# One half tile of a routed mixture of experts, run as a quarter tile in four groups of array columns

## The chip, the cores and the metric

The kernel runs on one core of a Trainium2 chip. The metric is the device time of one execution in microseconds; the time before is the median of three runs. Profiles show one execution each. The engines are named as in the profile: PE (matrix products) with PEld (its weight loads), DVE (vector), ACT (scalar), POOL (gather and scatter here) and SP (which sends the weight loads).

## The reference

A linear attention over 4 sequences of 768 tokens with 8 heads of 64 makes x, of 3,072 rows of 512. Each token then goes to one of 8 experts, and its row passes through that expert's two layers. What matters here, cut:

```python
logits = np.einsum('bsd,de->bse', x, w_gate)
local_gate = 1.0 / (1.0 + np.exp(-np.einsum('bsd,de->bse', x, w_local).squeeze(-1)))
for b in range(B):
    prev_e = -1
    for s in range(S):
        fresh_e = int(np.argmax(logits[b, s]))
        if s == 0 or local_gate[b, s] < 0.5:
            e = fresh_e
        else:
            e = prev_e if prev_e >= 0 else fresh_e
        prev_e = e
        ...
        h = np.maximum(x[b, s] @ w1[e], 0.0)
        out[b, s] = p[e] * (h @ w2[e])
```

w1[e] is 512 x 1024 and w2[e] is 1024 x 512, all in f32. p[e] is the token's softmax probability of its expert. The inputs come from a fixed seed, so the number of tokens of each expert is the same in every run. The kernel finds it on the chip all the same.

## The kernel before

**Attention and routing.** The first part goes through 24 steps, one for each block of 128 tokens (loop at L762). Each step computes scores (L181), the part from the running state (L216), the mix (L230), the update of the state (L242) and the rows of x (L258), which go to the DRAM tensor x_dram. Between the steps stand small pieces of other work, listed by step in the table extras (L732); constants_1 to constants_5 prepare constants there. A constant of this kind is dupb (L333): it copies rows 0 to 63 of a table to both halves of the 128 partitions when it is used as the stationary operand of a matmul.

**Tiles of tokens.** Tokens of one expert are collected in tiles of up to 128 rows. Five first tiles are taken while attention still runs. For the rest, other_tiles (L517) divides what each expert has left into pairs of tiles (256 rows, computed by a scheme of seven products in place of eight, L916), full tiles (128 rows) and half tiles (at most 64 rows). tokens_to_other_tiles (L544) gives each token its place and writes three numbers, arms[0] to arms[2]: how many later pairs, full tiles and half tiles there are. brought (L563) and by_slots (L580) turn places into row indices, gates and expert numbers for each tile. The numbers are read into registers (number, L727), and branches on them choose the code that runs (L1197 for the half tiles; the first arm, for three half tiles, falls through).

**A half tile.** Its rows come by a gather (ahead_half). turned_half (L1015) transposes them on PE. hidden_of_half (L1023) computes the first layer with the 64 tokens as the stationary operand, so that a matmul fills 64 of the 128 columns of the array; the outputs are cut in two, and the two cuts use columns 0 to 63 and 64 to 127. hidden_turned (L1033) transposes the result, and output_of_half (L1041) does the second layer in the same way, 8 steps of two matmuls. A row of 512 outputs so lies in two partitions, 256 values in each. both_halves (L612) prepares for this the scatter indices sidxh (two for each token) and the gates gateh. The scatter views out as rows of 256.

**Where half tiles run.** They have no stage of their own: hooks_of_halves (L1055) hangs their four steps into the first two pairs. With three half tiles, half 0 takes hooks 7 to 10 of pair 0, half 1 hooks 0 to 3 of pair 1, and half 2 hooks 7 to 10 of pair 1. Their weights have a set of buffers, w1t[2] and w2t[2]. The weights of the next half tile are sent by SP after the present one's last step, each layer once its reader on PE is done:

```python
            def end():
                output_of_half(h, now["ht"])
                if h + 1 < n:
                    weights_of(G2 + h + 1, 2)
```

**Order.** The orders of PE, DVE and SP are those of the program text (manual_schedule, L1105); each engine works through its own list and waits for what an instruction needs. Around the counts that order is: hiddens(2) and other_tiles, tokens_to_other_tiles, y of tile 2 (L724), brought (L568 and L577), then on PE by_slots (L587), which reads what L577 wrote. Constants written at steps 1 to 7 lie in ints, a region that the weights take later.

## Time and profile before

| measure | value |
|---|---|
| runs | 464.11, 515.61 and 462.61 us, median 464.11 |
| profiled execution | 462.59 us, of which the span from first to last instruction 460.4 |
| first half tile: L1018, L1027, L1036, L1046 | 195.66 to 209.6 us, with the pair's products between |
| second and third half tile, L1027 starts | 219.36 and 240.21 us |
| after the half tiles: third pair, full tiles, later pairs | from about 260 us to the end |
| last matmul of the span | starts 451.13, lasts 1.89 us |
| DMA moved | 124.30 MB, mean 270 GB/s |

Reading it: rows of the profile name a source line, an engine and the tile written and read. A piece of the chain of waits has its start and its length in microseconds. In an answer about a tile, three durations are the shortest, the median and the longest in nanoseconds.

### The profile page before, as it was taken

The numbers are of one execution on the slowest core, as the hardware profiler recorded it, in microseconds if no ns is written. First come the engines' busy times: TensorE is split into PE (matmuls) and PEld (weight loads), VectorE is DVE, ScalarE is ACT, GpSimd is POOL, SyncE is SP. The second block draws the span as 40 slices with busy tenths as digits, with TensorE's granted clock in tenths as the row PEclk, the third lists the DMA queues.
The fourth block names the chain that finished last, engine by engine and source line by source line (L and its number), as shares of the span: only waits on it lengthen the run. The fifth ranks groups of instructions, "written<-read, shape, count | busy, mean of one in ns | idle before, by whom it ended". The sixth has DMA issues, their size and how long they took to land.

```text
span 460.4 us, 10348 instructions
## 1 busy us (share of the span) xinstructions
PE 443.7 (96%) x4295; PEld 368.1 (80%) x4295; DVE 260.3 (57%) x514; ACT 111.4 (24%) x262; POOL 109.8 (24%) x121
## 2 busy tenths in 40 slices
PE   8898998989999999999999999999999999999993
PEld 7676886777766876968686999677799999898992
DVE  5465775762159743744373685100386877867661
ACT  3365665532011101121121031011031211213020
POOL 4475664421010120214021302010003012020101
PEclk9999999999999999999999999999999999999998
DMA  7999998996989999699993699997043828380101
GB/s 273 411 421 375 352 314 285 383 406 256 361 291 346 305 379 345 263 400 395 400 335 115 197 403 325 359 326 282 17 182 94 313 82 290 137 275 1 52 3 50
DMA packets 42236, 124.30 MB, mean 270 GB/s; under 512 B 3132, under 2 KB 3132, under 8 KB 40256
## 3 DMA queue, kind: packets, MB, share of 16 engines
q1 hardware_dynamic: 34544, 103.83, 61.5%
q0 software_dynamic: 4464, 14.16, 8.4%
q10 hardware_dynamic: 3168, 5.51, 3.2%
q8 instruction: 37, 0.61, 0.5%
q14 instruction: 23, 0.19, 0.1%
HBM read 123.49 MB, written 12.98 MB: 296 GB/s over the span
## 4 chain that ended last, share of the span: by engine, by line
PE 68%; DMA 15%; DVE 8%; issue 6%; POOL 1%; POOLq 0%; SPq 0%; ACT 0%; DVEq 0%
DMA xg<-x_dram,gidx 11%; PE pk L698 10%; PE ps L692 9%; PE ps L901 9%; PE pk L906 9%; DMA inp<-in_qkv_dram 4%; PE po L901 4%; PE pl L906 4%; PE po L237 4%; PE ps L197 3%; PE pr L1046 2%; PE pr L1027 2%; PE pk L261 2%; PE po L684 2%; PE po L224 2%
## 5 line engine op out<-in xcount | busy, mean ns | idle before, releaser
L692 PEld LDWEIGHTS ps<-xt,w 128*128 128x128 f32 x512 | 58.2, 192 | 3.4 <-issue 2.6
L692 PE MATMUL ps<-xt,w 128*128 128x128 f32 x512 | 59.1, 276 | 0.3 <-DVE xt L679 0.3
L698 PE MATMUL pk<-w,h 128*128 128x512 f32 x128 | 56.3, 592 | 0.0
L698 PEld LDWEIGHTS pk<-w,h 128*128 128x128 f32 x128 | 23.7, 190 | 26.8 <-issue 26.8
L669 POOL DMA_INDIRECT xg<-x_dram,gidx x23 | 25.5, 1110 | 78.4 <-PE po L684 57.9
L201 DVE TENSOR_TENSOR sm<-ps,mask 128x512 f32<-128x512 f32 x46 | 29.6, 685 | 16.9 <-PE ps L197 16.8
L707 POOL DMA_INDIRECT out_dram<-y,sidx x14 | 14.7, 1050 | 83.0 <-DVE y L724 46.5
L901 PE MATMUL ps<-xs,s 128*128 128x128 f32 x256 | 31.3, 275 | 0.1
L901 PEld LDWEIGHTS ps<-xp,w 128*128 128x128 f32 x256 | 30.4, 192 | 1.2 <-issue 0.9
L901 PE MATMUL ps<-xp,w 128*128 128x128 f32 x256 | 31.3, 275 | 0.0
L694 ACT ACTIVATE h<-ps 128x512 f32<-128x512 f32 x16 | 9.6, 597 | 88.0 <-PE ps L692 88.0
L906 PE MATMUL pk<-w,h 128*128 128x256 f32 x128 | 30.3, 379 | 0.0
L906 PE MATMUL pk<-s,hsum 128*128 128x256 f32 x128 | 30.2, 379 | 0.0
L901 PEld LDWEIGHTS ps<-xs,s 128*128 128x128 f32 x256 | 29.9, 192 | 0.3 <-DVE xs L882 0.3
L172 POOL TENSOR_TENSOR qd<-inp,lamq 128x512 f32<-128x512 f32 x20 | 25.6, 1280 | 16.4 <-DMA inp<-in_qkv_dram 4.4
L716 POOL DMA_INDIRECT out_dram<-y,sidxp x8 | 8.0, 1004 | 86.3 <-DVE y L997 80.4
L237 PE MATMUL po<-sm,inp 128*64 128x128 f32 x384 | 27.7, 280 | 0.8 <-issue 0.6
L724 DVE TENSOR_SCALAR y<-pk,gate 128x512 f32<-128x512 f32 x8 | 6.0, 746 | 39.7 <-PE pk L698 33.7
L237 PEld LDWEIGHTS po<-sm,inp 128*64 128x64 f32 x384 | 21.1, 136 | 8.3 <-issue 6.8
L175 POOL TENSOR_TENSOR kd<-inp,rev 128x512 f32<-128x512 f32 x20 | 21.7, 1084 | 20.6 <-PE pk L251 8.8
L906 PEld LDWEIGHTS pk<-s,hsum 128*128 128x128 f32 x128 | 24.0, 190 | 3.1
L906 PEld LDWEIGHTS pk<-w,h 128*128 128x128 f32 x128 | 23.2, 190 | 2.5
(258 smaller groups left out, 747.1 us busy)
## 6 DMA issues: line engine op xcount, KB each, us to landing
w<-in_w_dram SPq DMA_DIRECT2D x43, 2048.0 KB, 9.9
inp<-in_qkv_dram SPq DMA_DIRECT2D x15, 1024.0 KB, 9.0
x_dram<-xn ACTq DMA_DIRECT2D x21, 256.0 KB, 7.7
inp<-in_qkv_dram SPq DMA_DIRECT2D x10, 512.0 KB, 11.2
inp<-in_qkv_dram SPq DMA_DIRECT2D x4, 768.0 KB, 7.8
w<-in_w_dram SPq DMA_DIRECT2D x4, 512.0 KB, 8.0
x_dram<-xn POOLq DMA_DIRECT2D x2, 256.0 KB, 6.7
xg<-x_dram,gidx POOLq DMA_INDIRECT x23, 6.9
```

What stands on the lines that cost most here:

```text
L172: nc.gpsimd.tensor_tensor(qd, x[:, 0].rearrange("p (a i) -> p a i", i=P), lamq, ALU.mult)
L175: nc.gpsimd.tensor_tensor(kd.rearrange("p (h d) -> p h d", d=DH), x[:, 3].rearrange("p (h d) -> p h d", d=DH), rev.unsqueeze(2).broadcast_ ...
L197: nc.tensor.matmul(ps[u][half, a, first:], lhsT=kt[rows, a, js], rhs=qt[rows, a, first:], start=True, stop=True, skip_group_check=True)
L201: nc.vector.tensor_tensor(sm[:, u], ps[u], mask[:, u], ALU.mult)
L237: nc.tensor.matmul(head(a, u), lhsT=vn[:, a, u], rhs=sm[:, u, a], start=(not c and a < 2), stop=True, skip_group_check=True)
L669: nc.gpsimd.indirect_dma_start(out=xg, out_offset=None, in_=x_dram[:n, :], in_offset=bass.IndirectOffsetOnAxis(ap=gidx[i][:, j:j + 1], axi ...
L692: nc.tensor.matmul(ph[:, j], lhsT=w1t[w][:, d, P * f:P * f + P], rhs=xtt[i][:, d], start=(d == 0), stop=(d == DT - 1))
L694: nc.scalar.activation(hq[half, i], ph, ACT.Relu)
L698: nc.tensor.matmul(pys[i], lhsT=hq[f // 4, i][:, f % 4], rhs=w2t[w][:, f], start=(f == 0), stop=(f == FT - 1))
L707: apart(nc.gpsimd.indirect_dma_start(out=out, out_offset=bass.IndirectOffsetOnAxis(ap=sidx[i][:, j:j + 1], axis=0), in_=y, in_offset=None, ...
L901: nc.tensor.matmul(to[:, m], lhsT=a[:, k, P * m:P * m + P], rhs=b[:, k], start=(new and not m and not k), stop=(k == 1), skip_group_check= ...
L906: nc.tensor.matmul(to, lhsT=a[:, f], rhs=b[:, f], start=(new and not f), stop=(f == FT // 2 - 1), skip_group_check=True)
```

## The change

When there are three half tiles and the first of them has at most 32 tokens, that first one runs as a quarter tile: the 32 tokens are the stationary operand of four groups of 32 array columns, and each group computes a quarter of the outputs. A row of outputs then lies in four partitions, 128 values in each. For this there are a constant dupq (rows 0 to 31 copied four times) and fourth (the number of the quarter), a ninth column of sidxh and gateh, and a number FIRST_SMALL = 9 in arms[2] that the branch tests first. The case of three half tiles with a larger first one moves to the list of the other arms. The functions of a half tile take a number n of column groups, 2 or 4.

```diff
+QP = P // 4
+FIRST_SMALL = E + 1
...
+    def constants_6():
+        for k in range(4):
+            nc.vector.tensor_copy(dupq[:, QP * k:QP * k + QP], ident[:, :QP])
+        row = ints[0][:, 2 * P:2 * P + 1]
+        nc.vector.tensor_scalar(row, row, P - QP, None, ALU.bitwise_and)
+        nc.vector.tensor_scalar(fourth, row, 1.0 / QP, None, ALU.mult)
...
-    sidxh = route.tile([P, E], U32, name="sidxh")
-    gateh = route.tile([P, E], F32, name="gateh")
+    sidxh = route.tile([P, E + 1], U32, name="sidxh")
+    gateh = route.tile([P, E + 1], F32, name="gateh")
...
             nc.vector.tensor_tensor_scan(ends[:, k], ones8, tiles[:, k], float(g), ALU.mult, ALU.add)
-
+        small = nows["small"] = act.tile([1, E], F32, name="small", bufs=1)
+        nc.vector.scalar_tensor_tensor(small, rest[0:1], float(QP), tiles[0:1, 2], ALU.is_le, ALU.mult)
+        nc.vector.scalar_tensor_tensor(small, ends[0:1, 2], float(G2 + 1), small, ALU.is_equal, ALU.mult)
...
-        for k, g in ((1, G1), (2, G2)):
-            nc.vector.tensor_scalar(arms[k], ends[0:1, k, E - 1:], -float(g), None, ALU.add)
+        nc.vector.tensor_scalar(arms[1], ends[0:1, 1, E - 1:], -float(G1), None, ALU.add)
+
+        kind = act.tile([1, 3], F32, name="kind", bufs=1)
+        nc.vector.tensor_reduce(kind[:, 0:1], nows["small"], axis=AX.X, op=ALU.add)
+        nc.vector.tensor_scalar(kind[:, 1:2], ends[0:1, 2, E - 1:], -float(G2), None, ALU.add)
+        nc.vector.tensor_scalar(kind[:, 2:3], kind[:, 1:2], 3.0, float(FIRST_SMALL - 3), ALU.is_equal, ALU.mult)
+        nc.vector.scalar_tensor_tensor(arms[2], kind[:, 2:3], kind[:, 0:1], kind[:, 1:2], ALU.mult, ALU.add)
...
-        nc.tensor.matmul(twin, lhsT=dupb, rhs=nows["few"].rearrange("p k g -> p (k g)"), start=True, stop=True,
-                         skip_group_check=True)
+        nc.tensor.matmul(twin[:, :, :E], lhsT=dupb, rhs=few, start=True, stop=True, skip_group_check=True)
+        nc.tensor.matmul(twin[:, :, E:], lhsT=dupq, rhs=few[:, :, 0:1], start=True, stop=True, skip_group_check=True)
...
-        nc.vector.scalar_tensor_tensor(sidxh, src[:, 0], 2.0, upper.broadcast_to([P, E]), ALU.mult, ALU.add)
+        nc.vector.scalar_tensor_tensor(sidxh[:, :E], src[:, 0, :E], 2.0, upper.broadcast_to([P, E]), ALU.mult, ALU.add)
+        nc.vector.scalar_tensor_tensor(sidxh[:, E:], src[:, 0, E:], 4.0, fourth, ALU.mult, ALU.add)
...
-        (1, 0): constants_1, (4, 1): constants_2, (5, 1): constants_3, (6, 1): constants_4, (7, 1): constants_5,
+        (1, 0): constants_1, (4, 1): constants_2, (5, 1): constants_3, (6, 1): constants_4, (7, 1): constants_5, (8, 1): constants_6,
...
+        w = F // n
         for d in range(DT):
-            for c in range(2):
-                nc.tensor.matmul(pr[HP * c:HP * c + HP], lhsT=xt[:, d], rhs=w1t[2][:, d, F // 2 * c:F // 2 * c + F // 2],
+            for c in range(n):
+                nc.tensor.matmul(pr[P // n * c:P // n * c + P // n, :w], lhsT=xt[:, d], rhs=w1t[2][:, d, w * c:w * c + w],
                                  start=(d == 0), stop=(d == DT - 1), skip_group_check=True)
...
+        k = FT // n
         pt = pg.tile([P, DT, P], F32, name="po1")
-        for j in range(DT):
+        for j in range(k):
             nc.tensor.transpose(pt[:, j], hs[:, P * j:P * j + P], ident)
...
         for f in range(FT):
-            for c in range(2):
-                nc.tensor.matmul(py[HP * c:HP * c + HP], lhsT=ht[:, f % DT, f // DT],
-                                 rhs=w2t[2][:, f, DM // 2 * c:DM // 2 * c + DM // 2],
+            for c in range(n):
+                nc.tensor.matmul(py[P // n * c:P // n * c + P // n], lhsT=ht[:, f % k, f // k],
+                                 rhs=w2t[2][:, f, w * c:w * c + w],
                                  start=(f == 0), stop=(f == FT - 1), skip_group_check=True)
...
-        with tc.If(halves == 3, preferred_fallthrough_block=True, label="halves") as cmp:
-            first_pairs(3)
+        with tc.If(halves == FIRST_SMALL, preferred_fallthrough_block=True, label="halves") as cmp:
+            first_pairs(3, 4)
             others()
         with cmp.Else():
-            one_of(halves, [4, 2, 5, 1, 6, 0, 7, 8], None, first_pairs)
+            one_of(halves, [3, 4, 2, 5, 1, 6, 0, 7, 8], None, first_pairs)
             others()
```

More of the change, by code (lines that the diff above doesn't have):

```diff
@@ L299 @@
     upper = const.tile([P, 1], F32, name="upper")
+    dupq = const.tile([P, P], BF16, name="dupq")
+    fourth = const.tile([P, 1], F32, name="fourth")
     ones8 = const.tile([P, E], F32, name="ones8")
@@ L612, in both_halves @@
     def both_halves():
-        twin = pl[:, :5 * E]
-        nc.tensor.matmul(twin, lhsT=dupb, rhs=nows["few"].rearrange("p k g -> p (k g)"), start=True, stop=True,
-                         skip_group_check=True)
-        got = act.tile([P, 5, E], F32, name="twin", bufs=1)
-        nc.vector.tensor_copy(got, twin.rearrange("p (k g) -> p k g", k=5))
-        src = act.tile([P, 2, E], F32, name="srch", bufs=1)
+        twin = pl[:, :5 * (E + 1)].rearrange("p (k g) -> p k g", k=5)
+        few = nows["few"]
+        nc.tensor.matmul(twin[:, :, :E], lhsT=dupb, rhs=few, start=True, stop=True, skip_group_check=True)
+        nc.tensor.matmul(twin[:, :, E:], lhsT=dupq, rhs=few[:, :, 0:1], start=True, stop=True, skip_group_check=True)
+        got = act.tile([P, 5, E + 1], F32, name="twin", bufs=1)
+        nc.vector.tensor_copy(got, twin)
+        src = act.tile([P, 2, E + 1], F32, name="srch", bufs=1)
         nc.vector.tensor_scalar(src[:, 0], got[:, 0], -float(P), 0.0, ALU.add, ALU.max)
@@ L1013, in ahead_half, with turned_part @@
         collect(xgh, 1, G2 - KA + h)
-    def turned_half():
+    def turned_part(n):
         pt = pg.tile([P, DT, P], F32, name="po1")
@@ L1018, in turned_half, with hidden_of_part @@
             nc.tensor.transpose(pt[:, d], xgh[:, P * d:P * d + P], ident)
-        xt = act.tile([P, DT, HP], F32, name="xth", bufs=1)
-        nc.vector.tensor_copy(xt, pt[:, :, :HP])
-        return xt
-    def hidden_of_half(xt):
+        xt = act.tile([P, DT, HP], F32, name="xth", bufs=1)[:, :, :P // n]
+        nc.vector.tensor_copy(xt, pt[:, :, :P // n])
+        return xt
+    def hidden_of_part(xt, n):
+        w = F // n
         for d in range(DT):
-            for c in range(2):
-                nc.tensor.matmul(pr[HP * c:HP * c + HP], lhsT=xt[:, d], rhs=w1t[2][:, d, F // 2 * c:F // 2 * c + F // 2],
+            for c in range(n):
+                nc.tensor.matmul(pr[P // n * c:P // n * c + P // n, :w], lhsT=xt[:, d], rhs=w1t[2][:, d, w * c:w * c + w],
@@ L1028, in hidden_of_half, with hidden_turned @@
                                  start=(d == 0), stop=(d == DT - 1), skip_group_check=True)
-        hs = act.tile([P, F // 2], F32, name="hs", bufs=1)
-        nc.scalar.activation(hs, pr, ACT.Relu)
-        return hs
-    def hidden_turned(hs):
+        hs = act.tile([P, F // 2], F32, name="hs", bufs=1)[:, :w]
+        nc.scalar.activation(hs, pr[:, :w], ACT.Relu)
+        return hs
+    def hidden_turned(hs, n):
+        k = FT // n
         pt = pg.tile([P, DT, P], F32, name="po1")
-        for j in range(DT):
+        for j in range(k):
@@ L1036, in hidden_turned, with output_of_part @@
             nc.tensor.transpose(pt[:, j], hs[:, P * j:P * j + P], ident)
-        ht = act.tile([P, DT, 2, HP], F32, name="hth", bufs=1)
-        nc.scalar.copy(ht.rearrange("p j c i -> p j (c i)"), pt)
-        return ht
-    def output_of_half(h, ht):
-        py = pr[:, :DM // 2]
+        ht = act.tile([P, DT, P], F32, name="hth", bufs=1)[:, :k]
+        nc.scalar.copy(ht, pt[:, :k])
+        return ht.rearrange("p j (c i) -> p j c i", c=n)
+    def output_of_part(h, ht, n):
+        w = DM // n
+        k = FT // n
+        py = pr[:, :w]
@@ L1044, in output_of_half @@
         for f in range(FT):
-            for c in range(2):
-                nc.tensor.matmul(py[HP * c:HP * c + HP], lhsT=ht[:, f % DT, f // DT],
-                                 rhs=w2t[2][:, f, DM // 2 * c:DM // 2 * c + DM // 2],
+            for c in range(n):
+                nc.tensor.matmul(py[P // n * c:P // n * c + P // n], lhsT=ht[:, f % k, f // k],
+                                 rhs=w2t[2][:, f, w * c:w * c + w],
                                  start=(f == 0), stop=(f == FT - 1), skip_group_check=True)
-        y = act.tile([P, DM // 2], F32, name="yh", bufs=1)
@@ L1050, in output_of_half @@
-        nc.vector.tensor_scalar(y, py, gateh[:, h:h + 1], None, ALU.mult)
-        apart(nc.gpsimd.indirect_dma_start(out=out.rearrange("n (c d) -> (n c) d", c=2),
-                                           out_offset=bass.IndirectOffsetOnAxis(ap=sidxh[:, h:h + 1], axis=0),
-                                           in_=y, in_offset=None, bounds_check=2 * N - 1, oob_is_err=False))
-    def hooks_of_halves(n):
+        y = act.tile([P, DM // 2], F32, name="yh", bufs=1)[:, :w]
+        j = h if n == 2 else E
@@ L1057, in hooks_of_halves @@
+        nc.vector.tensor_scalar(y, py, gateh[:, j:j + 1], None, ALU.mult)
+        apart(nc.gpsimd.indirect_dma_start(out=out.rearrange("n (c d) -> (n c) d", c=n),
+                                           out_offset=bass.IndirectOffsetOnAxis(ap=sidxh[:, j:j + 1], axis=0),
+                                           in_=y, in_offset=None, bounds_check=n * N - 1, oob_is_err=False))
+    def hooks_of_halves(n, first):
         now = {}
@@ L1063, in steps @@
         def steps(h):
+            cols = 2 if h else first
             def start():
-                now["xt"] = turned_half()
+                now["xt"] = turned_part(cols)
                 if h + 1 < n:
@@ L1069, in middle @@
             def middle():
-                now["hs"] = hidden_of_half(now["xt"])
+                now["hs"] = hidden_of_part(now["xt"], cols)
             def turn():
-                now["ht"] = hidden_turned(now["hs"])
+                now["ht"] = hidden_turned(now["hs"], cols)
             def end():
-                output_of_half(h, now["ht"])
+                output_of_part(h, now["ht"], cols)
                 if h + 1 < n:
@@ L1105 @@
     with tc.manual_schedule(engines={PE, DVE, SP}):
-        more, fulls, halves = (number(k, n) for k, n in enumerate((PMAX - PMIN + 1, E + 1, E + 1)))
+        more, fulls, halves = (number(k, n) for k, n in enumerate((PMAX - PMIN + 1, E + 1, FIRST_SMALL + 1)))
         weights_of(KA, w_of(0), (2,))
@@ L1119, with first_pairs @@
         written(4, 0)
-        def first_pairs(n):
-            hooks = hooks_of_halves(n)
+        def first_pairs(n, first=2):
+            hooks = hooks_of_halves(n, first)
             def loads():
```

## The prediction

> **What bounds the kernel now.** I read the page first: busy shares, then slices.

> ```profile
> PE 443.7 (96%) x4295; PEld 368.1 (80%) x4295; DVE 260.3 (57%) x514; ACT 111.4 (24%) x262; POOL 109.8 (24%) x121
> ...
> PE   8898998989999999999999999999999999999993
> ...
> PEclk9999999999999999999999999999999999999998
> DMA  7999998996989999699993699997043828380101
> ```

> TensorE is busy in almost every slice at full clock, so a microsecond less of matmul is a microsecond less of span, unless something else is late in its place. DMA is the candidate: slices 15 to 20 (about 173 to 242 us), where the half tiles run, are nearly full. Next, the chain of waits from 195 to 211 us, which is the first half tile inside the first pair.

> ```profile
> 195.82 0.44 PE po L1018 x4
> 196.26 1.73 PE pk L906 x8
> 197.99 3.58 PE pr L1027 x16
> 201.57 0.59 PE po L684 x4
> 202.16 1.73 PE pl L906 x8
> 203.89 0.44 PE po L1036 x4
> 204.32 1.73 PE pk L906 x8
> 206.05 3.60 PE pr L1046 x32
> ```

> Every piece is TensorE, without a gap: transposes of the rows (L1018), first product (L1027), transposes of the hidden values (L1036), second product (L1046), with work of the pair between. An f32 matmul leaves two records, so x16 is 8 matmuls. No vector or scalar piece stands here, so what this tile saves on PE is saved. Then I read the chain and timeline around 140 to 157 us, where the tile counts are made:

> ```profile
> 149.51 0.13 DVE arm L559
> 149.64 0.12 DVE arm L561 x2
> 149.76 0.66 DVE y L724
> 150.42 1.03 DVE hit L568
> 151.45 0.02 issue
> 151.47 5.20 DVE w L577 x5
> 156.66 0.04 issue
> 156.71 2.17 PE pr L587 x24
> ```

> ```profile
> 156.71 2.17 PE L587 MATMUL pr<-w,lane 128*128 128x190 bf16 x24 [0.28 <-DVE w L577]
> ```

> Here VectorE is the chain, and PE already waits 0.28 us for it. Anything added to VectorE ahead of L577 is paid by PE at once.

> **Does the quarter run?** The reference's routing on its seeded inputs gives 410, 373, 371, 423, 434, 362, 354, 345 tokens for the experts. With 128 of each of experts 0 to 4 in the first five tiles and 256 of each in pairs, experts 0, 3 and 4 keep 26, 39 and 50; experts 5 to 7 take the full tiles. So three half tiles (the trace has three of each half group), and the first has 26 tokens, at most 32: arms[2] becomes 9 and the quarter arm runs.

> **First product.** Now 8 matmuls of 512 columns in two groups of 64 array columns. A full-width f32 matmul of 512 columns takes 0.86 us (L698, 16 records in 6.87 us), so 8 would need 6.87; two side by side took 3.58. After: 16 matmuls of 256 columns, each 0.43 us alone (L906, 8 records in 1.73), in four groups: 16 x 0.43 / 4 = 1.72, plus the fill that the half shows (3.58 - 3.44 = 0.14 to 0.18): 1.88. Gain 1.70. That four groups run side by side is seen in the gates, one matmul of 512 columns for each 32-column group:

> ```profile
> L275 PEld LDWEIGHTS pl<-xc,wgt x48: 106/108/109, 23.5 to 106.6; 128*32 128x32 f32 x48
> L275 PE MATMUL pl<-xc,wgt x48: 592/605/617, 23.5 to 107.0; 128*32 128x512 f32 x48
> ```

> On the chain one set (8 records) is 0.99 us at 39.82; four alone would be 3.44. That row never reloads a group's weights while its neighbours run; the quarter does, eight times in its second product. The half does it with two groups and loses nothing.

> **Second product.** Now 16 matmuls of 256 columns, 3.60 us; after, 32 of 128 columns in four groups. Alone each is 0.22 us (L692, 64 records in 7.14), 7.1 in all, / 4 = 1.79, plus fill: 1.90. Gain 1.70. The doubt is how fast instructions go in: 64 matmul records in 1.8 us is 28 ns each, each with a weight load. The nearest row is from_state:

> ```profile
> 48.51 0.45 PE po L224 x16
> ```

> 16 records in 0.45 us, 28 ns each. [...] L275 shows 3.44 / 0.99 = 3.5 including its fill, so mine (6.9 / 1.88 = 3.7, fill spread over more steps) leans on the row[...].

> **Transposes.** L1036: 4 become 2, each 0.147 (L684, four in 0.59): 0.29 gained. L1018 stays. Copies and gating off the path (relu 0.60, hth 0.59, yh 0.48, all on smaller tiles) get shorter; PE has a product of 1.73 us between each and its reader, so they bring nothing. The scatter (POOL, 1.02 us issue) stays one instruction with half the bytes.

> **Added on VectorE ahead of L577.** In the timeline independent small operations start about 0.08 apart, dependent ones 0.20:

> ```profile
> 140.14 0.17 DVE L530 SCALAR_TENSOR_TENSOR other<-other 128x8 f32<-128x8 f32 x1
> 140.34 0.17 DVE L531 TENSOR_SCALAR other<-other 128x8 f32<-128x8 f32 x1
> 140.42 0.32 DVE L533 TENSOR_TENSOR_SCAN ends<-ones,other 128x8 f32<-128x8 f32 x3
> ```

> small: one independent, one dependent, 0.28. kind: a reduction (0.08 to 0.15), an independent step, then two dependent ones, in place of one arm: net 0.5. Together 0.8 us, no cover, since PE already waits there. Behind it on VectorE stand y (L724), hit, w; POOL's gathers (160.5, 161.8) and SP's weight loads of 159.4 and 159.7 move with it, as do their users. Bounds: 0.5 (all pipelined at 0.08) to 1.3 (all at 0.2).

> **both_halves.** One more bf16 matmul with its load: L413 and L414 start 0.04 apart; 0.05 on PE. VectorE's extra operation (0.2) is covered: it sits idle 7.3 us before L881 at 181.8. Without that cover: 0.2.

> **constants_6.** Four casts of 128x32 and two single-column steps follow L254 at 44.1:

> ```profile
> 43.72 0.42 DVE L254 TENSOR_TENSOR kv<-pk,kv 128x256 f32<-128x256 f32 x1 [2.98 <-PE pk L251]
> 44.66 1.29 DVE L201 TENSOR_TENSOR sm<-ps,mask 128x512 f32<-128x512 f32 x2 [0.52 <-PE ps L197]
> ```

> Nearest is L335 (0.79 and 0.18, the long one beside a POOL operation) and L336 (0.21). About 1.0 us, of which 0.5 is the idle before L201. Behind it are the scores, then fresh_experts; the first reader on PE is L386 at 48.89, whose input L378 ends at 48.33. So 0.5 late costs 0 to 0.1; I take 0.1, bounds 0 and 0.6. The halves branch still falls through in its first arm, and no queue is passed by a moved step: counted from the tile's start, w1t[2] comes free 1.7 us earlier and w2t[2] 3.7.

> **Sum.** -1.70 - 1.70 - 0.29 + 0.80 + 0.05 + 0.10 = -2.75 us. The profiled execution took 462.59 (span 460.4 and 2.2 around it): 459.8. The runs were 462.61, 464.11 and 515.61; the median lies 1.5 above the profiled one, which would make 461.4. Two executions agree at 462.6, so I say 460.3.

> **Rivals.**
> Weights late: half 1's w1 is sent at 201.61, when L1027 frees the buffer, and read at 219.4; the interval shrinks from 17.8 to 15.8 us. Loads of 2048 KB land 9.9 us after issue in the median, so DMA can even stay as late as now (211.5) and miss nothing (needed at 215.7 at the earliest). Against: two loads around 160 us took 19.5 and 18.2, queued behind others. At 18.2 PE would wait 2.4 and leave 0.35: 462.2.
> [...]
> VectorE stretch worse than summed, 1.3 and 0.6 for the constants: gain 1.75, 460.8.
> Covers better than summed (0.5 and 0): 459.5.
> The other side: the four groups don't run side by side once each reloads its weights. In series the products take 6.9 and 7.1 us in place of 3.58 and 3.60; +6.8 - 0.29 + 0.95 = +7.5: 470.1, slower than before. It decides from an overlap of 2.1 of four downward (each product above 3.26 us). For: L275 does no reload. Against: the half's pair overlaps 1.92 of two with reloads.

> **Numbers.** Main case 0.60, weights 0.08, issue 0.13, VectorE 0.10, covers 0.05, series 0.04. The range 458.5 to 463.8 takes in all but the series case, with 1.5 us for where the median of a few runs falls. About 2% (9.3 us) is what a measurement of this kernel can tell from no change; no case reaches it on either side, and what I leave is for effects the profile doesn't show: faster 0.03, same 0.95, slower 0.02.

> **What would show it.** First product: 32 records in about 1.9 us at 195 to 200. Second: 64 in about 1.9; [...]near 7 series. L1036 x2. PE's idle before L587 from 0.28 to about 1.1, with L577 starting 0.8 later. L386 at most 0.1 later. No PE wait before half 1's L1027. The pairs and full tiles after 260 us keep their lengths and start about 2.7 earlier. I am wrong if the products take over 2.6 us each, or if a wait of over 1 us stands where the chain had none.

## The result, and the profile after

The changed kernel takes 460.65 us in the median of 13 runs (458.73 to 463.36) against 463.52 us before: a ratio of 0.9929, 95% interval 0.9904 to 0.9955. By the ratio that is 3.3 us less, between 2.1 and 4.4; the two medians differ by 2.87. It is under one percent, but clear of noise. One run of before, 515.61 us, was in a slow state and does not enter the ratio. The forecast was 460.3, by a sum of 2.75 us less.

The profiled execution took 462.44 us with a span of 460.7, and so hardly differs from the profiled one of before (462.59 and 460.4). The profiles show how both can be true. First the page of the changed kernel, its header and busy shares:

```profile
span 460.7 us, 10452 instructions
...
PE 442.0 (96%) x4342; PEld 368.2 (80%) x4342; DVE 261.8 (57%) x526; ACT 110.7 (24%) x262; POOL 110.0 (24%) x121
```

TensorE has 47 more records and 1.7 us less of busy time. The busy time alone decides little: second profiles of both kernels have 445.1 us before and 440.1 after. Next the chain of waits through the first half tile, which is now the quarter tile (start, length, what). L1048 is the first product, L1058 the transposes of the hidden values, L1070 the second product.

```profile
199.82 0.44 PE po L1038 x4
200.26 1.73 PE pk L926 x8
201.99 1.86 PE pr L1048 x32
203.85 0.59 PE po L704 x4
204.44 1.73 PE pl L926 x8
206.17 0.22 PE po L1058 x2
206.38 1.73 PE pk L926 x8
208.11 1.89 PE pr L1070 x64
210.00 0.59 PE po L704 x4
```

Read it against the chain shown in the prediction: 3.58 became 1.86, 0.44 became 0.22, 3.60 became 1.89, and the pair's own pieces between them kept their lengths. From the start of the first product to the end of the second it was 11.67 us and is 8.01: 3.66 less, all on the chain.

Then the price. The chain ahead of by_slots, and by_slots' line of the timeline with TensorE's wait in brackets:

```profile
153.07 0.05 DVE arm L572
153.13 0.06 DVE arm L573
153.19 0.07 DVE kind L576
153.25 0.07 DVE kind L577
153.33 0.02 issue
153.35 0.15 DVE kind L578
153.50 0.02 issue
153.53 0.04 DVE arm L579
153.56 0.10 issue
153.66 0.73 DVE y L744
```

```profile
160.68 2.17 PE L605 MATMUL pr<-w,lane 128*128 128x190 bf16 x24 [1.02 <-DVE w L595]
```

The wait of 0.28 us has become one of 1.02. The two rows of small stand earlier, at 143.88 and 144.05.

What hides all this in the profiled pair stands ahead of it. The transposes of the first expert tile (its turn, in the table), the first work behind attention that every version has, start at 104.20 in the changed kernel and at 100.97 before, in the chain 3.23 us later:

```profile
104.20 0.60 PE pr L698 x4
```

From there to the end of the span the changed kernel takes 356.50 us and the one before 359.43: 2.93 less. So the comparison needs two numbers for each profile, where this piece starts and how long the rest takes (the span less that start). All profiles of this study:

| kernel | turn of the first expert tile starts | from there to the end |
|---|---|---|
| before, two profiles | 100.97, 101.67 | 359.43, 359.43 |
| after, two profiles | 104.20, 98.95 | 356.50, 356.55 |
| additions only, two profiles | 101.69, 101.01 | 360.21, 360.19 |
| small and kind late | 102.15 | 355.75 |
| all counts and y late, two profiles | 101.80, 102.63 | 355.30, 355.47 |
| groups in turn | 103.33 | 363.17 |
| columns split | 102.43 | 356.57 |
| runs of two | 102.56 | 356.64 |
| before with constants_6 | 103.33 | 359.57 |

The second column scatters over 5 us, for one and the same kernel too; the third repeats within 0.2 us. What the change does inside the span is read from the third.

There is also a piece outside the span, the time of a run less its span. In every run of the kernel before with a span on record it is 2.06 to 2.24 us (median 2.12), and the same with constants_6 added. In every run of the versions with the whole change or all its additions it is 1.68 to 1.86 (median 1.75). So 2.9 us inside and 0.37 outside make the 3.3 of the ratio. The 0.37 comes with the additions other than constants_6, since the version without the quarter has it too; the cause was not looked for.

Inside and outside together give each version a ratio to compare with its runs, if the attention stage takes the same in the mean. The measured ratio agrees within its interval for the changed kernel, all counts late, groups in turn, constants_6 and the second run of the additions. It does not for the first run of the additions (1.0042, where 1.0009 is expected) and for small and kind late (0.9939, where 0.9913 is). Both come from the same series of runs, and so does groups in turn, which agrees.

### The profile page after: what moved, and what is told of

Read it like the earlier page. It is cut to its first block, busy times and chain, and to the rows that moved or that the text cites. A ratio compares the mean times of both kernels' runs of the same rounds, so it can differ in the third digit from the quotient of the medians.

```text
span 460.7 us, 10452 instructions
## 1 busy us (share of the span) xinstructions
PE 442.0 (96%) x4342; PEld 368.2 (80%) x4342; DVE 261.8 (57%) x526; ACT 110.7 (24%) x262; POOL 110.0 (24%) x121
## 4 chain that ended last, share of the span: by engine, by line
PE 70%; DMA 12%; DVE 9%; issue 7%; POOL 1%; POOLq 0%; ACT 0%; DVEq 0%
DMA xg<-x_dram,gidx 11%; PE pk L718 10%; PE ps L712 9%; PE ps L921 9%; PE pk L926 9%; PE po L239 5%; PE po L921 4%; PE ps L199 4%; PE pl L926 4%; PE pk L263 2%; PE pk L253 2%; PE pr L1070 2%; PE pr L1048 2%; PE po L704 2%; PE po L226 2%
```

## Experiments

**Before, a second profile.** No edit.

> The kernel before, profiled a second time. In the first pair of profiles everything up to the first matmul of the expert stage stood 3.2 us later after the change (pr L678 at 100.97 before, L698 at 104.20 after), though only constants_6 was added there. Theory A (the attention stage differs from execution to execution[...]): this piece starts anywhere from 100 to 105 us here too, at least 0.5 us away from 100.97. Theory B (constants_6 shifts that stage): it starts within 0.5 us of 100.97.

The turn starts at 101.67, 0.7 us from the first profile, which favours A, weakly. The rest of the table says more: one kernel, the changed one, started its turn at 104.20 and at 98.95. The last lies outside the 100 to 105 that I had allowed; the scatter is wider than stated. Whether constants_6 adds a small shift of its own can't be seen in such a scatter; the run with constants_6 alone, below, answers that.

**The additions without the quarter** (two runs).

```diff
-            first_pairs(3, 4)
+            first_pairs(3, 2)
```

> All additions of the change are kept and the branch of the ninth kind is taken, but its first half tile runs in two column groups as before. Theory A (the gain is the two products and two transposes of the quarter, 3.7 us, and the additions cost 0.8 to 0.95): slower than the kernel before by 0.8 to 0.95 us (ratio 1.002), 3.7 us slower than the changed kernel; products 3.58 and 3.60 us, TensorE waits about 1.0 us ahead of by_slots. Rival (the gain comes from what the branch or the layout of the code does, not from the quarter): as fast as the changed kernel, ratio 0.993.

Measured: ratio 1.0042 (1.0021 to 1.0063). The chain of this run has the products of a half tile back:

```profile
199.49 3.58 PE pr L1048 x16
203.07 0.59 PE po L704 x4
203.66 1.73 PE pl L926 x8
205.38 0.44 PE po L1058 x4
205.82 1.73 PE pk L926 x8
207.55 3.60 PE pr L1070 x32
```

and the wait ahead of by_slots stays:

```profile
158.18 2.16 PE L605 MATMUL pr<-w,lane 128*128 128x190 bf16 x24 [1.03 <-DVE w L595]
```

The rival is out: without the quarter nothing is gained. The table gives the additions 0.78 us and the quarter 3.71 (360.21 - 356.50). The runs, however, gave 1.9 us for the additions, with even the lower end of the interval, 1.0 us, above what the profile shows. So I repeated it.

> The additions without the quarter, once more, beside the changed kernel and the version with all counts late on one chip. By the profiles the stage behind attention is 0.8 us longer than before, but its runs were 1.9 us slower (1.0 to 2.9). Theory A (the attention stage varies by up to 3 us from execution to execution, and the runs of one call don't average that out): ratio nearer to 1.002 this time, interval with 1.0018 in it. Rival (the additions cost a further 1 us that the profiles don't show): ratio 1.004 again.

Measured: ratio 1.0008 (0.9988 to 1.0027), with 1.0018 in it, and 360.19 us from the turn to the end. The stage behind attention repeats to 0.02 us, while the ratio moved by 0.0034 between the two series of runs. Rival and first ratio are not confirmed. With the 0.37 us that the additions save outside the span they should cost 0.4 us in all, a ratio of 1.0009, and that is what the second series has. What the first series had more of isn't known.

**Constants_6 alone.** The kernel before, with

```diff
+        (8, 1): constants_6,
```

and its function, but no reader.

> The kernel before with nothing added but constants_6, whose results nobody reads. Theory A (covered: VectorE has 0.5 us free there and the next reader on TensorE has slack): four steps of the attention from the first L197 group after it keep their 10.95 us, ratio 1.000. Rival (the additions cost more in time, 1.9 us in the run with additions only, than the 0.8 that the stage behind attention shows, because of constants_6): the four steps take 0.5 us or more longer, ratio 1.002.

Measured: ratio 0.9993 (0.9971 to 1.0016). The chain's score pieces after it, and those of before, start and length:

```profile
45.07 0.81 PE ps L198 x24
49.00 0.81 PE ps L198 x24
52.55 0.81 PE ps L198 x24
56.02 0.81 PE ps L198 x24
```

```profile
43.77 0.81 PE ps L197 x24
47.70 0.81 PE ps L197 x24
51.24 0.81 PE ps L197 x24
54.72 0.81 PE ps L197 x24
```

10.95 us from the first to the fourth in both (three steps lie between them, where the expectation says four). On this stretch the constants cost nothing; the ratio alone would leave room for a loss of up to 0.7 us. Their cover is visible on VectorE, in the timeline of the changed kernel:

```profile
45.57 0.61 DVE L344 CAST dupq<-ident 128x32 bf16<-128x32 f32 x4
46.10 0.14 DVE L346 TENSOR_SCALAR w<-w 128x1 int32<-128x1 int32 x1
46.27 0.15 DVE L347 TENSOR_SCALAR fourth<-w 128x1 f32<-128x1 int32 x1
46.34 1.28 DVE L203 TENSOR_TENSOR sm<-ps,mask 128x512 f32<-128x512 f32 x2
```

0.8 us of work in the place of 0.5 us of idle time; sm starts 0.16 us later against its scores, and its reader on TensorE comes a step later.

**The counts late.** small and kind move behind brought, where VectorE waited for by_slots anyway (2.26 us ahead of its copy of the result, L609, in the changed kernel).

```diff
         brought(1, (0, 1, 2, 3, 4))
+        kind_of_first()
```

kind_of_first holds the six operations taken out of other_tiles and tokens_to_other_tiles.

> The changed kernel, with the four operations of kind and the two of small moved behind brought, where VectorE waits 2.26 us for by_slots. Theory A (the additions cost because VectorE is the chain ahead of by_slots): TensorE's wait ahead of by_slots falls from 1.02 to 0.25 to 0.35 us, the piece between the lane of the last tokens (VectorE) and by_slots is 0.7 to 0.8 us shorter than in the changed kernel, and the time is about 0.75 us below it (ratio to before 0.9915). Rival (the wait is set by something else, a load or the hidden product): the wait stays at 1.0 us.

```profile
157.72 0.15 DVE L576 SCALAR_TENSOR_TENSOR small<-other 1x8 f32<-1x8 f32 x1
157.85 2.17 PE L608 MATMUL pr<-w,lane 128*128 128x190 bf16 x24 [0.25 <-DVE w L598]
```

The wait is 0.25 us, and the rest takes 355.75 us, 0.75 less than in the changed kernel. The ratio, 0.9939 (0.9916 to 0.9963), does not show it: it is no lower than that of the changed kernel, and the 0.9915 that A had lies just outside its interval. By the profile A holds; by the runs it is not confirmed.

**All counts and y late** (two runs). In addition arms[0], arms[1] and the gating of the third tile go behind brought.

```diff
-        finished(2)
+        output(0, 0)
         weights(4)
         brought(1, (0, 1, 2, 3, 4))
         kind_of_first()
+        written(2, 0)
```

> The version with the late counts, with all three arms and the gating of the third tile (y, 0.66 us) behind brought too, so that VectorE is about 0.8 us earlier at by_slots. Theory A (with the additions and y gone from the chain, TensorE's own hidden product is the limit): TensorE's wait ahead of by_slots is 0, and from the turn of the first expert tile to the end the kernel takes 0.25 us less than the version with late counts (355.75 us): 355.5, against 359.4 and 359.5 in the two profiles of before; ratio to before about 0.991. Rival (what is moved behind brought then delays the copy of by_slots' result or the scatters): from that point on 0.5 us or more is lost again, 356 or above.

```profile
157.09 2.17 PE L608 MATMUL pr<-w,lane 128*128 128x190 bf16 x24
...
157.82 0.75 DVE L747 TENSOR_SCALAR y<-pk,gate 128x512 f32<-128x512 f32 x1 [0.23 <-issue]
...
159.29 0.36 DVE L612 COPY got<-pr 128x190 f32<-128x190 f32 x1 [0.72 <-PE pr L608]
```

TensorE no longer waits there, and VectorE still has 0.72 us to spare before it copies the result. 355.30 us, as expected (355.5). Ratio 0.9907 (0.9874 to 0.9940). Once more beside the changed kernel:

> The changed kernel once more. From the turn of the first expert tile (first transpose into pr) to the end the first profile had 356.5 us, before 359.4 and 359.5. Theory A (what the change does lies behind attention and repeats): 356.5 within 0.3 us again, wherever the turn starts; ratio 0.991 to 0.996. Rival (the stage behind attention also varies): the difference to 356.5 is over 0.5 us.

> The version with all counts late once more, beside the changed kernel. Theory A: 1.0 us below the changed kernel by the stage behind attention (355.4 us against 356.5), ratio to before 0.989 to 0.993. Rival (what was saved ahead of by_slots is lost in the executions that are not profiled): no faster than the changed kernel.

The changed kernel: 0.9928 (0.9909 to 0.9947), 356.55 us behind the turn. The late version: 0.9902 (0.9864 to 0.9940), 355.47 us. In the median it took 459.6 us (6 runs) against 460.2 (22 runs). By the stage that repeats it is 1.1 us faster than the changed kernel and 4.0 to 4.1 faster than the one before, so it beats both there. Against the changed kernel the runs don't decide, since the intervals of the ratios overlap.

**The groups in turn.** Same instructions, other order, in both products of the quarter:

```diff
-        for d in range(DT):
-            for c in range(n):
+        for c, d in [(c, d) for c in range(4) for d in range(DT)] if n == 4 else [(c, d) for d in range(DT) for c in range(n)]:
+            if True:
...
```

> The changed kernel, with the loop over the four column groups outside the loop over the contraction in both products of the quarter tile, so that one group's matmuls follow each other. Same instructions, same weight loads, other order. Theory A (the gain rests on neighbouring matmuls going to different column groups): they run in series, 6.9 us for the first product and 7.1 for the second in place of 1.86 and 1.89, and the kernel is about 10 us slower than the changed one, some 7 us slower than the one before (ratio 1.015). Rival (a matmul with 32 stationary columns is cheaper in itself, whatever stands beside it): both products stay at about 1.9 us.

```profile
201.15 4.52 PE pr L1048 x32
...
209.93 5.88 PE pr L1070 x64
```

Ratio 1.0069 (1.0045 to 1.0093). The rival is out: 32 stationary columns are not cheap in themselves, and with this order the change is a loss. A has the direction but not the size: 4.52 and 5.88 us, not 6.9 and 7.1. There are three changes of group in each product. Each saved (6.88 - 4.52) / 3 = 0.79 us in the first and (7.1 - 5.88) / 3 = 0.41 us in the second: 3.7 records in both, at 0.215 and 0.11 us a record. So, by an estimate from these times, the last four records or so of one group run beside the first four of the next. The trace of the first product fits it. Cut into half microseconds from 201.15 on, it has 3, 5, 8, 8, 8, 8, 8, 5 and 3 records of the product in them (one that touches two is counted in both): few for 1 us at each end, where one group stands alone, and more for the 2.5 us between. If so, then runs of four records in one group should cost little. That can be tried:

**Runs of two.** In the second product, two matmuls (four records) in one group before the next group.

```diff
-        for f in range(FT):
-            for c in range(n):
+        run = 2 if n == 4 else 1
+        for f, c in [(f + i, c) for f in range(0, FT, run) for c in range(n) for i in range(run)]:
+            if True:
```

> The changed kernel, with two matmuls (4 records) in the same column group before the next group, in the second product only. The run with the groups in turn took 4.52 and 5.88 us in place of 6.9 and 7.1: at each change of group some 3.7 records were saved[...]. Theory A[...] the product takes 1.9 to 2.2 us. Rival ([...]a second matmul for a busy group holds up everything behind it): the product takes 16 x 0.22 = 3.4 us or more.

```profile
206.50 1.95 PE pr L1071 x64
```

1.95 us in place of 1.89: no strict alternation is needed. The rival (a busy group holds up what stands behind it at once) is out for runs of four records. How the engine does it was not looked for.

**The columns split.** Each matmul of the second product cut in two, so twice the instructions for the same work of the array.

```diff
+        parts = 2 if n == 4 else 1
+        v = w // parts
         for f in range(FT):
-            for c in range(n):
-                nc.tensor.matmul(py[P // n * c:P // n * c + P // n], lhsT=ht[:, f % k, f // k],
-                                 rhs=w2t[2][:, f, w * c:w * c + w],
...
+            for q in range(parts):
+                for c in range(n):
+                    nc.tensor.matmul(py[P // n * c:P // n * c + P // n, v * q:v * q + v], lhsT=ht[:, f % k, f // k],
+                                     rhs=w2t[2][:, f, w * c + v * q:w * c + v * q + v],
...
```

> The changed kernel, with each matmul of the quarter's second product cut into two of 64 columns: 64 matmuls (128 records) in place of 32, the same work of the array. Theory A (28 ns per record was near the limit at which instructions go in): the product takes 128 x 28 ns = 3.6 us in place of 1.89. Rival (the array was the limit, instructions have room): it stays at about 1.9 us. Between the two lies the limit itself, divided by 128.

```profile
206.37 1.92 PE pr L1073 x128
```

128 records with as many weight loads in 1.92 us, 15 ns each. So at 28 ns a record the rate at which instructions go in was not the limit: twice the records for the same work took 0.03 us more. (The outputs of this version differ from the reference's, with a relative error of 0.023; the cause was not looked for. The version serves only to time these instructions.)

## Why the prediction was right, and where it was off

The terms of the sum, on the chain:

| term | forecast | measured |
|---|---|---|
| first product | -1.70 | -1.72 (3.58 to 1.86) |
| second product | -1.70 | -1.71 (3.60 to 1.89) |
| transposes of the hidden values | -0.29 | -0.22 (0.44 to 0.22) |
| VectorE ahead of L577 | +0.80 | +0.74 (wait 0.28 to 1.02) |
| both_halves on PE | +0.05 | about +0.03 (L634 to L635) |
| constants_6 | +0.10 | 0.0 (10.95 in both) |
| sum | -2.75 | -2.9 (359.43 to 356.50) |
| outside the span | 0 | -0.37 (2.12 to 1.75) |
| whole | -2.75 | -3.3 (ratio 0.9929) |

The products are right to 0.02 us. They were worked out from rows of the same profile: what a full-width matmul with as many moving columns takes, how close to two at once the half's two groups came, and that the gates run four groups at once (8 records in 0.99 us, where 3.44 is worked out for one after another). That four groups also run so with new weights for each matmul no row showed; the forecast took it over from two groups, and it held. The doubt that I kept, instructions at 28 ns each, was no limit at all: with the columns split, twice as many took 1.92 us. The 0.13 for the issue case was the author's estimate, and no run showed such a bound.

The transposes were mis-sized: I divided a group of four with its tail (0.59) by four. On the chain one takes 0.11, as L1036's own line had it (four in 0.44), and the two removed brought 0.22.

The term on VectorE rests on how far apart small operations start, and was right to 0.06 us. That PE pays for it in full is shown by the late counts: with the additions out of the way 0.75 us came back.

The rivals. Late weights: the interval shrank as computed, w1 of half 1 is sent at 203.94 and read at 219.70, 15.8 us later. The loads sent between 199 and 240 us did land later, 12.3 us after issue in the median where it was 9.8 before, but no wait came: in the chain the first product of half 1 follows without a gap.

```profile
217.99 1.79 PE ps L921 x16
219.78 3.58 PE pr L1048 x16
```

Series: true only with another order of the loop. That order cost 3.7 us against the kernel before, by the table (363.17 - 359.43), where the forecast of that rival had 7.5, since the groups overlap at their changes even then (4.52 and 5.88 us, not 6.9 and 7.1).

One statement failed: that pairs and full tiles after 260 us would start 2.7 us earlier. In the first profile they start 0.3 later, because the attention stage ran 3.2 us longer in that execution. I had named no such scatter, and read the stage as if it were the same in every run. Over 13 runs it evens out: their ratio is what the stage behind attention and the piece outside the span add up to.

That 460.3 came so near to 460.65 is in part luck. The forecast put the base between two values, at 463.05, and 13 runs have 463.52; and it carried the 2.2 us outside the span over unchanged, where 0.37 went away. The first error made the time too low, the second too high. The other cases of the forecast (460.8, 459.5, 462.2) start from 462.59 instead, the profiled execution; from there the main case is 459.8. The 2% that the forecast took as the least to be told from no change was too much: the interval of these runs spans 0.5%.

## What to carry to other kernels

Few rows in a tile need not fill the array: with the loop over column groups innermost, or in runs of two matmuls, four groups of 32 columns took about a quarter of what the second product is worked out to take with one matmul after another (1.89 and 1.95 us of 7.1), and a loop in the other order lost more than the change gains. Small counting operations can be placed where their engine waits anyway: these six, of 0.13 to 0.21 us each, made TensorE wait 0.74 us longer where they were put, and not at all a few lines later. Where runs scatter by more than the change is worth, find a piece that all versions share, compare from there, and check that what lies outside it adds up to the time of the runs.

## What was not expected of the hardware

```profile
70.56 0.11 PE pk L253 x2
70.67 1.37 issue
72.03 0.68 PE pk L253 x14
```

```profile
68.87 0.77 PE pk L253 x16
```

What TensorE waits for there the chain doesn't say, and it was not tried.
